# Earlier weight fetches, fewer unread constant products and a direct split of PSUM in the opening of a fused attention and two-layer kernel

## The chip, the cores and the metric

The kernel runs on one core of a Trainium2 chip. The metric is the device time of one execution in microseconds; the figure for the kernel before is the median of three runs. Engines are called as the profile calls them: PE is TensorE, PEld its weight loads, DVE is VectorE, ACT is ScalarE, POOL is GpSimd, and SP is SyncE, which here issues nearly all DMAs.

## What is computed

Causal attention with a bias, then two token-wise layers. Inputs q, k and v are 4 x 8 heads x 576 tokens x 64; the layers are 512 wide with 2048 hidden units, over 2304 tokens, all float32.

```python
bias = -(cum[:, :, :, None] - cum[:, :, None, :])        # cum = cumsum(max(s, 0))
scores = np.where(causal, -1e9, q @ k.T / 8 + np.minimum(bias, 0.0))
attn = softmax(scores)
x = (attn @ v)                       # heads side by side: 2304 x 512
h = x @ w1_in;  x = (h * sigmoid(1.702 * h)) @ w1_out
h = x @ w2_in;  out = (s * max(h, 0)**2 + b) @ w2_out
```

## The kernel before, in words

Float32 operands are split into a rounded part (`hi`, fp32r) and the remainder (`lo`); a product of two split operands is three matmuls. Tokens go in eight units (320 or 256 tokens of one batch). While PE works through the first layer of one unit, the attention of the next unit is woven between its matmuls. The first unit has nothing to be woven into, so its attention stands alone at the start of the program: this opening is where the change lies.

The opening (L540 to L558) runs in steps 0 to 9. In step n PE makes, in this order, the scores of head n in three chunks (`qk`, into `ps`, L311), the values of head n-2 (`pv`, into `po`, L370), and the transposes of head n-1 in two groups (`t`, into `pst`, L349). Behind them DVE masks the scores (L317), ACT takes the exponential (L323), DVE and ACT or POOL normalise (L327, L328, L121, L123), and ACT copies the transposes into `ph` (L353). Only plain float32 is used for the first unit (heads 0 to 7); head 8 is the first of unit 1, and its scores are made from split operands `hi` (L288) and `lo`.

After pv of each head, ACT copies `po` to `xraw` (L384); four `xraw` tiles hold eight heads, two heads each. `split_x` (L424, L425) turns an `xraw` tile into `xT`, whose two planes are the rounded part (ACT) and the remainder (DVE). Just before pv of head 7 PE begins three hidden blocks of the first layer with three of the four `xT` tiles (`h_begin`, 27 matmuls into `ph1`, L438); after it, the last three matmuls of each follow as soon as the fourth tile is there.

Between the pieces of a step PE multiplies a constant tile, `warm`, by itself (`keep_busy`, L201, 128 x 512 bf16 into `bank`); nobody reads the result. `FIRST` such products stand at the start, `FILL` and `EARLY_FILL` say how many precede each piece of a step, and two more stand ahead of each of the hidden blocks 3 to 7 (L458).

Meanwhile the weights come: 16 blocks of `w1i` and then 16 of `w1o`, each 512 KB, by SP (L135). Each one takes ACT and DVE: a sign pass on ACT (L146), a merge of two passes on DVE (L156, L158), and a split (ACT L166, DVE L167). `w1i` has 16 buffers, `w1o` three, so the fourth `w1o` is fetched when the first is split. `next_w1i` and the three calls of `fetch_w` at L555 fix where in SP's order these fetches stand. SP's order and PE's are written out by hand in the opening; those of ACT, DVE and POOL are set by a scheduler when the program is built. All engines execute in order.

SP and ACT issue DMAs on eight completion semaphores in rotation (`DMAHW0` to `DMAHW7` in the order of instructions), and an issue waits there for the DMA that used its semaphore last.

## Time and profile before

| | us |
|---|---|
| median of 3 runs | 1040.61 (1039.55 to 1043.46) |
| the profiled execution | 1039.54 |
| its span | 1037.8 |
| PE busy | 1012.0 (98% of the span) |
| ACT, DVE, POOL busy | 628.1, 609.4, 344.1 |

The 1.7 us between time and span lie around the profiled program. PE is the bound of the whole, so what it loses (idle time, and time in which its clock is granted at half) is what there is to win: in the first 100 us PE is busy for 84.7 us, in the remaining 937.8 us for all but about 10 us. "Idle before" in the rows is time in which an engine had nothing to run, with the instruction whose end released it.

### The profile page before, as it was taken

The numbers are of one execution on the slowest core, as the hardware profiler recorded it, in microseconds if no ns is written. First come the engines' busy times: TensorE is split into PE (matmuls) and PEld (weight loads), VectorE is DVE, ScalarE is ACT, GpSimd is POOL, SyncE is SP. The second block draws the span as 40 slices with busy tenths as digits, with TensorE's granted clock in tenths as the row PEclk, the third lists the DMA queues.
The fourth block names the chain that finished last, engine by engine and source line by source line (L and its number), as shares of the span: only waits on it lengthen the run. The fifth ranks groups of instructions, "written<-read, shape, count | busy, mean of one in ns | idle before, by whom it ended". The sixth has DMA issues, their size and how long they took to land.

```text
span 1037.8 us, 18019 instructions
## 1 busy us (share of the span) xinstructions
PE 1012.0 (98%) x6434; PEld 929.3 (90%) x6434; DVE 609.4 (59%) x1379; ACT 628.1 (61%) x1364; POOL 344.1 (33%) x381
## 2 busy tenths in 40 slices
PE   8978999999999999999999999999999999999998
PEld 3447999999989999999999999899989899999997
DVE  5869766465456677677776565666474334532232
ACT  5968767567538767767767555666455344543342
POOL 1215445345326445445535332011043342311010
PEclk9988999999999999999999999999999999999999
DMA  6766222222022222232222077765126437353321
GB/s 221 241 200 201 66 84 72 57 84 64 8 96 82 83 87 86 73 102 72 86 91 69 15 274 239 253 218 199 46 93 243 158 117 243 111 203 104 119 71 62
DMA packets 52881, 129.60 MB, mean 125 GB/s; under 512 B 7068, under 2 KB 19480, under 8 KB 52792
## 3 DMA queue, kind: packets, MB, share of 16 engines
q1 hardware_dynamic: 52584, 128.32, 37.5%
q8 instruction: 51, 0.84, 0.3%
q14 instruction: 38, 0.31, 0.1%
q10 hardware_dynamic: 208, 0.13, 0.0%
HBM read 95.45 MB, written 28.90 MB: 120 GB/s over the span
## 4 chain that ended last, share of the span: by engine, by line
PE 87%; DVE 4%; DMA 3%; ACT 2%; POOL 1%; issue 1%; SPq 0%; POOLq 0%; DVEq 0%; ACTq 0%
PE py L788 18%; PE ph L438 17%; PE py L480 17%; PE sum_p L762 6%; PE pst L349 5%; PE ph L838 5%; PE ps L311 5%; PE po L376 4%; PE sum_r L762 3%; PE py L729 2%; PE sum_q L762 2%; PE bank L201 1%; DMA pair<-w1o 1%; PE po L370 1%; DMA pair<-w1i 1%
## 5 line engine op out<-in xcount | busy, mean ns | idle before, releaser
L438 PE MATMUL ph<-xT,wi 128*128 128x320 f32 (+1 forms) x1536 | 244.8, 303 | 4.9 <-ACT xT L424 2.0
L788 PE MATMUL py<-wo,g 128*128 128x512 f32 x864 | 223.1, 394 | 0.7 <-DVE g L825 0.7
L438 PEld LDWEIGHTS ph<-xT,wi 128*128 128x128 f32 x1536 | 215.1, 191 | 7.5 <-ACT xT L424 2.2
L480 PE MATMUL py<-g,wo 128*128 128x320 f32 (+1 forms) x1344 | 215.4, 304 | 0.2
L480 PEld LDWEIGHTS py<-g,wo 128*128 128x128 f32 x1344 | 188.1, 189 | 1.2 <-POOL g L467 0.6
L788 PEld LDWEIGHTS py<-wo,g 128*128 128x128 f32 x864 | 160.6, 188 | 26.3 <-DVE g L825 1.0
L467 POOL TENSOR_TENSOR g<-th,g 128x320 fp32r<-128x320 f32 (+1 forms) x128 | 111.1, 869 | 135.1 <-ACT g L466 127.5
L323 ACT ACTIVATE x<-x,m 64x64 f32<-64x64 f32 (+2 forms) x160 | 89.3, 558 | 48.0 <-DVE m L317 47.1
L291 POOL TENSOR_TENSOR lo<-raw,hi 64x576 fp32r<-64x576 f32 (+1 forms) x56 | 68.3, 1220 | 149.5 <-PE ps L311 84.7
L317 DVE CUSTOM_DVE_ANT_0 x<-ps,mask 64x64 f32<-64x64 f32 (+2 forms) x160 | 68.3, 427 | 59.5 <-PE ps L311 58.1
L825 POOL TENSOR_TENSOR g<-odd,g 128x768 fp32r<-128x768 f32 x16 | 30.5, 1907 | 183.3 <-ACT g L822 183.3
L355 ACT ACTIVATE ph<-pst 64x256 fp32r<-64x256 f32 (+2 forms) x144 | 68.4, 476 | 35.6 <-PE pst L349 34.2
L349 PE MATMUL pst<-ident,x 128*128 128x128 f32 (+2 forms) x480 | 82.0, 274 | 1.3 <-DVE ph L358 1.3
L762 PE MATMUL sum_p<-xs,part 128*128 128x384 f32 x384 | 78.5, 339 | 1.4 <-ACT e L860 1.2
L358 DVE TENSOR_TENSOR pl<-pst,ph 128x512 fp32r<-128x512 f32 (+1 forms) x88 | 53.3, 605 | 38.9 <-ACT ph L355 38.4
L762 PEld LDWEIGHTS sum_p<-xs,part 128*128 128x128 f32 x384 | 69.2, 188 | 7.4 <-ACT e L860 1.7
L860 ACT ACTIVATE e<-sum_p 128x384 f32<-128x384 f32 x48 | 23.5, 489 | 84.9 <-PE sum_p L762 84.9
L462 DVE SCALAR_TENSOR_TENSOR th<-th,ph 128x320 f32<-128x320 f32 (+1 forms) x128 | 57.7, 450 | 26.9 <-ACT th L461 25.5
L123 POOL TENSOR_SCALAR x<-x,tot 64x64 f32<-64x64 f32 (+1 forms) x96 | 47.4, 501 | 76.8 <-DVE tot L328 52.3
L466 ACT ACTIVATE g<-th 128x320 fp32r<-128x320 f32 (+1 forms) x128 | 56.1, 438 | 26.3 <-DVE th L462 26.0
L838 PE MATMUL ph<-xs,wi 128*128 128x384 f32 x384 | 71.8, 335 | 0.0
L461 ACT ACTIVATE th<-ph 128x320 f32<-128x320 f32 (+1 forms) x128 | 51.7, 404 | 31.8 <-PE ph L438 30.2
(111 smaller groups left out, 1684.1 us busy)
## 6 DMA issues: line engine op xcount, KB each, us to landing
part<-parts_d SPq DMA_DIRECT2D x32, 512.0 KB
raw<-qkT SPq DMA_DIRECT2D x32, 416.0 KB
pair<-w1i SPq DMA_DIRECT2D x16, 512.0 KB
pair<-w1o SPq DMA_DIRECT2D x16, 512.0 KB
pair<-w2i SPq DMA_DIRECT2D x16, 512.0 KB
pair<-w2o SPq DMA_DIRECT2D x16, 512.0 KB
parts_d<-part SPq DMA_DIRECT2D x16, 512.0 KB
raw<-qkT SPq DMA_DIRECT2D x24, 320.0 KB
```

Of the source, the lines that this page charges most:

```text
L291: nc.gpsimd.tensor_tensor(lo[:D, kc], raw[:D, kc], f32(hi[:D, kc]), ALU.subtract)
L317: nc.vector.tensor_tensor_reduce(out=x[:w, j0:j1], in0=ps[:w, : j1 - j0], in1=mask[:w, WIDE - a0 + j0 : WIDE - a0 + j1], scale=-1.0 / ROOT ...
L323: nc.scalar.activation(x[:w, :a1], x[:w, :a1], AF.Exp, bias=least, scale=-1.0, accum_out=tot[:w, c : c + 1])
L349: nc.tensor.transpose(ps[: j1 - j0, at : at + a1 - a0], t["x"][c][: a1 - a0, j0:j1], ident[: a1 - a0, : a1 - a0])
L355: nc.scalar.activation(t["ph"][:rows, base:end], ps[:rows, :m], AF.Copy)
L438: nc.tensor.matmul(ph[:, :n], wi[f][:, a, cc * P : (cc + 1) * P], x[cc][:, b, :n], start=(k == 0), stop=(k == 3 * NC - 1),)
L462: nc.vector.scalar_tensor_tensor(out=th[:, :n], in0=th[:, :n], scalar=1.0, in1=ph[:, :n], op0=ALU.add, op1=ALU.mult)
L467: nc.gpsimd.tensor_tensor(g[:, 1, :n], th[:, :n], f32(g[:, 0, :n]), ALU.subtract)
L480: nc.tensor.matmul(py[:, :n], wo[f][:, a, wc], g_t[ui, f][:, b, :n], start=(k == 0), stop=(k == 3 * G - 1))
L762: nc.tensor.matmul(ps[:, :N2], w[:, a, c0 : c0 + P], x[kind, k // 3][:, b, :], start=(first and k == 0), stop=(k == 5), skip_group_check=n ...
L788: nc.tensor.matmul(y_sums[t], g2[f % 2][:, a, t * P : (t + 1) * P], wo2[f][:, b, :], start=(first and k == 0), stop=end)
L838: nc.tensor.matmul(ps[:, :N2], wi2[f][:, a, cc * P : (cc + 1) * P], x[f"{cc // 2 + 1}{n + 1}", cc % 2][:, b, :], start=(k == 0), stop=(k = ...
```

## The change

The diff has three parts. `w1i` blocks are fetched one fewer in the set-up and one more after step 0, and the first three `w1o` blocks two steps sooner, after step 5 where they stood after step 7. The constant products are redistributed: 18 in step 1 (20 before), 6 in each step from 2 to 7 (9 before), 6 in steps 8 and 9 (8 before), none ahead of the hidden blocks 3 to 7 (10 before), and 10 after pv of head 7, ahead of the last three matmuls of the first hidden block, into a bank of the transposes: 22 fewer in all, 100 where there were 122. And the values of heads 0 to 7 go from PSUM straight into `xT`: ACT writes the rounded part of 64 x 320, DVE subtracts it from `po`; `xraw` and `split_x` are left out for this unit.

```diff
--- before.py
+++ after.py
@@ -30,7 +30,7 @@
 
 QK_AT, PV_AT, T_AT = (0.05, 0.35), 0.45, (0.55, 0.45)
 SPAN = 0.98
-FIRST, FILL, EARLY_FILL = 30, {"qk": 1, "pv": 2, "t": 2}, {(1, "qk"): 4, (1, "t"): 4}
+FIRST, LAST, FILL, EARLY_FILL = 30, 10, {"qk": (0, 1, 1), "pv": (2,), "t": (1, 1)}, {"qk": (6, 4, 2), "t": (3, 3)}
 EARLY = 1.0
 AHEAD, LEAD = 2, 4
 
@@ -187,7 +187,7 @@
 
         heads = {}
         vs = {}
-        xraw = {}
+        xraw, x0 = {}, []
 
         warm = gp.tile([P, 2 * NMAX], F32, tag="g", name="warm")[:, : C // 2]
         nc.vector.memset(warm, 1.0)
@@ -212,7 +212,7 @@
             raw = t["parts"][0][0]
             nc.sync.dma_start(raw[D + 2 : R, t["kc"]], minus[:2, : u.i1])
             nc.sync.dma_start(raw[D : D + 2, t["qc"]], root[:2, u.i0 : u.i1])
-            next_w1i(2)
+            next_w1i(1)
             for k in range(2):
                 nc.sync.dma_start(rows_d[0, :, 2 + k, :], minus)
                 nc.sync.dma_start(rows_d[1, :, k, :], root)
@@ -375,14 +375,18 @@
                     rhs = t[part][:, at : at + u.n - i]
                     nc.tensor.matmul(po[:, i : u.n], lhs, rhs, start=start, stop=(j == last and part == "ph"))
                     start = False
+            m0 = D * (h % 2)
+            if n < H:
+                if h % 2 == 0:
+                    x0.append(xp.tile([P, 2, NMAX], F32R, tag="xT", name="xT", bufs=4))
+                hi, lo = (x0[-1][m0 : m0 + D, k, : u.n] for k in range(2))
+                nc.scalar.activation(hi, po[:D, : u.n], AF.Copy)
+                nc.vector.tensor_tensor(lo, po[:D, : u.n], f32(hi), ALU.subtract)
+                return
             if h % 2 == 0:
                 xraw[n // H, h // 2] = xp.tile([P, NMAX], F32, tag="xraw", name="xraw")
             x = xraw[n // H, h // 2]
-            m0 = D * (h % 2)
             part = x[m0 : m0 + D, : u.n]
-            if n < H:
-                nc.scalar.activation(part, po[:D, : u.n], AF.Copy)
-                return
             nc.scalar.activation(part, po[D - m0 : 2 * D - m0, : u.n], AF.Copy)
             nc.vector.tensor_tensor(part, po[m0 : m0 + D, : u.n], part, ALU.add)
 
@@ -450,12 +454,12 @@
         def h_item(ui, f, x, between=None):
             n = units[ui].n
             if (ui, f) in begun:
+                if f == 0:
+                    keep_busy(LAST, psT.tile([P, 512], F32, tag="t", name="bank"))
                 ph = begun.pop((ui, f))
                 yield from h_sum(ph, n, f, x, range(NC - 1, NC))
             else:
                 ph = psM.tile([P, 512], F32, tag="m", name="ph1")
-                if ui == 0 and f < G:
-                    keep_busy(2, ph)
                 yield from h_sum(ph, n, f, x, range(NC))
             th = gp.tile([P, NMAX], F32, tag="th", name="th", bufs=2)
             nc.scalar.activation(th[:, :n], ph[:, :n], AF.Tanh, scale=0.851)
@@ -531,7 +535,7 @@
 
         with tc.tile_pool(name="half0", bufs=1, side="right") as pool, tc.manual_schedule(engines={PE}):
             attention_pool(pool, B * H, 0)
-            x0, first_wo = [], []
+            first_wo = []
 
             def next_w1i(n):
                 for f in range(len(wi), min(NF, len(wi) + n)):
@@ -543,15 +547,14 @@
                 for step in range(H + 2):
                     for item in attention_items(step):
                         if item[2] < H and (0, 0) not in begun:
-                            keep_busy(FILL.get(item[1], 0) if step > 1 else EARLY_FILL.get((step, item[1]), 0))
+                            keep_busy((FILL if step > 1 else EARLY_FILL)[item[1]][item[3]] if step else 0)
                         if item[2] == H - 1 and item[1] == "pv":
-                            x0 += [split_x(0, cc) for cc in range(NC - 1)]
                             for f in range(3):
-                                h_begin(0, f, x0)
+                                h_begin(0, f, x0[: NC - 1])
                         if item[2] < H:
                             attend(item)
-                    next_w1i(2)
-                    if step == H - 1:
+                    next_w1i(2 if step else 3)
+                    if step == H - 3:
                         first_wo.extend(fetch_w((pool, "pair", 3), w1o, f) for f in range(3))
                     if step == 1:
                         nc.sync.dma_start(s_sb, s2.partition_broadcast(P))
```

What this does to the instruction orders is shown at three places. In SP's order of the set-up, with the semaphores that each row waits for, before (`pair` is the buffer of a weight block, `raw` that of a head's q and k with the rows of the cumulative sums, `rows_d` their store in DRAM):

```order
L214 DMA raw_156<-root_152 2x320
L135 DMA pair_162<-w1i 128x1024
L135 DMA pair_170<-w1i 128x1024
L217 DMA rows_d_81<-minus_154 32x576
L218 DMA rows_d_81<-root_152 32x576 [waits DMAHW1_49]
L217 DMA rows_d_81<-minus_154 32x576 [waits DMAHW3_49]
L218 DMA rows_d_81<-root_152 32x576 [waits DMAHW4_49]
L230 DMA raw_156<-high_187 1x16x20 [waits DMAHW5_49,DVE_49]
L231 DMA raw_156<-high_187 1x16x20 [waits DMAHW6_49]
L233 DMA rows_d_81<-high_187 32x576 [waits DMAHW7_49]
```

The same place in the changed kernel:

```order
L214 DMA raw_156<-root_152 2x320
L135 DMA pair_162<-w1i 128x1024
L217 DMA rows_d_81<-minus_154 32x576
L218 DMA rows_d_81<-root_152 32x576
L217 DMA rows_d_81<-minus_154 32x576 [waits DMAHW1_49]
L218 DMA rows_d_81<-root_152 32x576 [waits DMAHW3_49]
L230 DMA raw_156<-high_179 1x16x20 [waits DMAHW4_49,DVE_49]
L231 DMA raw_156<-high_179 1x16x20 [waits DMAHW5_49]
L233 DMA rows_d_81<-high_179 32x576 [waits DMAHW6_49]
```

The second weight block has left this stretch, and the two rows from `high` wait for semaphores one place earlier: the first now for a small copy, the second for the first weight block, and none for a second block.

In SP's order after step 5 the piece of the difference with the first `w1o` blocks reads as follows; the row behind them fetches head 7:

```order
+L135 DMA pair<-w1i 128x1024 x2
+L135 DMA pair<-w1o 128x1024 x3
 L268 DMA raw<-qkT 64x640
 L264 DMA raw<-rows_d 4x320
```

The three blocks now stand ahead of the fetches of heads 7, 8 and 9 and of the last two `w1i` blocks.

On ACT, the rows of step 7 of the kernel before that end with the copies of head 6's transposes (`ph`), for which pv of head 6 waits (`hi` here is head 9's, the last row of `pair` ahead of `ph` the sign pass of the first `w1o` block):

```order
L323 ACTIVATE x_683,tot3_74<-x_683,m_686 64x64 [waits DVE_49]
L166 ACTIVATE wi15_664<-pair_659 128x512 [waits DVE_49]
L323 ACTIVATE x_690,tot3_74<-x_690,m_693 128x192 [waits DVE_49]
L323 ACTIVATE x_697,tot3_74<-x_697,m_700 128x320 [waits DVE_49]
L121 ACTIVATE x_617<-x_617,tot2_73 128x320 [waits DVE_49,Activation_49]
L121 ACTIVATE hi_841<-raw_839 128x640 [waits DMAHW1_49]
L384 ACTIVATE xraw_634<-po_710 64x320 [waits PE_49]
L121 ACTIVATE x_697<-x_697,tot3_74 128x320 [waits DVE_49,Activation_49]
L146 ACTIVATE pair_730<-pair_730 128x512 [waits DMAHW3_49]
L353 ACTIVATE ph_717<-pst_718 64x320 [waits PE_49]
L424 ACTIVATE xT_767<-xraw_634 128x320 [waits Activation_49]
L353 ACTIVATE ph_717<-pst_725 128x384 [waits PE_49]
```

And of the changed kernel (`pair_863` is the fourth `w1o` block):

```order
L121 ACTIVATE x_612<-x_612,tot2_73 128x320 [waits DVE_49,Activation_49]
L323 ACTIVATE x_676,tot3_74<-x_676,m_679 64x64 [waits DVE_49]
L166 ACTIVATE wi14_650<-pair_645 128x512 [waits DVE_49]
L323 ACTIVATE x_683,tot3_74<-x_683,m_686 128x192 [waits DVE_49]
L166 ACTIVATE wi15_658<-pair_653 128x512 [waits DVE_49]
L323 ACTIVATE x_690,tot3_74<-x_690,m_693 128x320 [waits DVE_49]
L121 ACTIVATE hi_826<-raw_824 128x640 [waits DMAHW4_49]
L383 ACTIVATE xT_629<-po_703 64x320 [waits PE_49]
L353 ACTIVATE ph_710<-pst_711 64x320 [waits PE_49]
L146 ACTIVATE pair_863<-pair_863 128x512 [waits DMAHW6_49]
L121 ACTIVATE x_690<-x_690,tot3_74 128x320 [waits DVE_49,Activation_49]
L353 ACTIVATE ph_710<-pst_717 128x384 [waits PE_49]
```

A sign pass of a `w1o` block still stands between the two copies; the splits of the first three blocks have moved ahead of this place.

## Rows read from the trace of the kernel before

**Rows 1.** busy time in stretches: us, PE, PEld, DVE, ACT, POOL busy, clock, DMA

```profile
15.00:20.00 5.00, 4.79 (x16) 2.60 (x17) 1.78 (x7) 2.08 (x7) 0.35 (x1) 0.66 0.97 336
...
25.00:45.00 20.00, 20.00 (x99) 10.25 (x98) 16.73 (x53) 19.93 (x53) 2.96 (x6) 1.00 0.81 263
...
60.00:65.00 5.00, 4.20 (x11) 1.52 (x12) 4.59 (x10) 4.30 (x9) 0.00 (x0) 0.50 0.30 120
...
75.00:80.00 5.00, 4.69 (x21) 4.21 (x22) 4.07 (x10) 3.45 (x9) 1.04 (x1) 0.66 0.63 211
...
85.00:90.00 5.00, 2.92 (x20) 2.33 (x18) 4.76 (x9) 3.81 (x10) 2.95 (x4) 1.00 0.75 268
...
95.00:100.00 5.00, 3.15 (x22) 2.80 (x20) 4.88 (x13) 4.53 (x12) 1.24 (x3) 1.00 0.57 172
```

**Rows 2.** timelines of SP, DVE and PE, set-up and step 1

```profile
9.57 0.52 SPq L231 DMA_DIRECT2D raw<-high  x1
...
8.02 0.43 DVE L156 TENSOR_SCALAR pair<-pair 128x512 uint32<-128x512 uint32 x1 [2.20 <-DMA pair<-w1i]
...
1.31 8.41 PE L201 MATMUL bank<-warm 128*128 128x512 bf16 x30 [1.31 <-DVE warm L193]
...
15.21 0.44 PE L311 MATMUL ps<-raw 68*64 68x64 f32 x2 [1.53 <-DMA raw<-rows_d]
```

**Rows 3.** the chain: start, duration, what; a DMA and constant products

```profile
4.70 4.85 DMA pair<-w1i
...
24.26 0.43 PE bank L201 x2
...
63.59 0.97 PE bank L201 x2
```

**Rows 4.** timeline of PE: the first scores of heads 3 and 4

```profile
28.12 0.33 PE L311 MATMUL ps<-raw 68*64 68x64 f32 x2
...
33.72 0.33 PE L311 MATMUL ps<-raw 68*64 68x64 f32 x2
```

**Rows 5.** timeline of ACT: start, duration, line, [idle before <-releaser]

```profile
24.38 0.34 ACT L323 ACTIVATE x<-x,m 64x64 f32<-64x64 f32 x1
...
28.14 0.69 ACT L146 ACTIVATE pair<-pair 128x512 f32<-128x512 f32 x1
...
28.69 0.57 ACT L121 ACTIVATE x<-x,tot 128x320 f32<-128x320 f32 x1
...
56.74 0.74 ACT L121 ACTIVATE hi<-raw 128x640 fp32r<-128x640 f32 x1 [1.42 <-DMA raw<-qkT]
...
59.76 0.68 ACT L146 ACTIVATE pair<-pair 128x512 f32<-128x512 f32 x1 [1.24 <-DMA pair<-w1o]
...
61.01 0.47 ACT L353 ACTIVATE ph<-pst 128x384 f32<-128x384 f32 x1
```

**Rows 6.** timeline of SP: fetch of head 9 and the first w1o blocks

```profile
53.23 0.33 SPq L272 DMA_DIRECT2D raw<-qkT  x1
...
54.67 1.52 SPq L135 DMA_DIRECT2D pair<-w1o  x3
```

**Rows 7.** timeline of PE: pv of heads 6 and 7 and what follows

```profile
60.80 2.79 PE L370 MATMUL po<-ph,vraw 64*64 64x320 f32 x6 [3.45 <-ACT ph L353]
...
71.00 1.54 PE L370 MATMUL po<-ph,vraw 64*64 64x320 f32 x6
...
74.55 0.41 PE L438 MATMUL ph<-xT,wi 128*128 128x320 f32 x1 [2.00 <-ACT xT L424]
...
75.31 0.99 PE L438 MATMUL ph<-xT,wi 128*128 128x320 f32 x5 [0.36 <-DVE xT L425]
```

**Rows 8.** single lines: durations in ns, minimum/median/maximum

```profile
L424 ACT ACTIVATE xT<-xraw x32: 401/435/473, 35.0 to 598.3; 128x320 fp32r<-128x320 f32 x16, 128x256 fp32r<-128x256 f32 x16
...
L387 DVE TENSOR_TENSOR xraw<-po,xraw x56: 396/427/495, 106.3 to 597.3; 64x256 f32<-64x256 f32 x32, 64x320 f32<-64x320 f32 x24
```

**Rows 9.** the weight buffers: DVE's split of a w1o block

```profile
L167 DVE TENSOR_TENSOR wo<-pair,wo x16: 662/692/1519, 63.3 to 111.2; 128x512 fp32r<-128x512 f32 x16
```

## The prediction, made before the changed kernel ran

> **What bounds the kernel now.** I read the busy times first: PE fills 98% of the span, so only what PE loses counts, and nearly all of that lies in the first 105 us. The busy time in stretches [rows 1] shows it twice: as idle time of PE (2.1 of 5 us from 85 on, 1.8 of 5 from 95 on), and in the column of the clock, 0.66, 0.50 and 0.66 in the stretches from 15, 60 and 75 us, where a part or all of the time ran at 1.2 instead of 2.4 GHz. From 25 to 45 us PE is busy for 20.00 us of 20 and at full clock, but so is ACT, for 19.93: two engines are full at once, and a part of PE's work there is constant products.
>
> Next I read who PE waits for. It waits 1.53 us for head 1's rows at 15.21 [rows 2], 3.45 us for ACT's copy of head 6's transposes at 60.80, and 2.00 and 0.36 us for the last tile of `xT` at 74.55 and 75.31 [rows 7]. Each of these waits ends just before, or within, a stretch of low clock.
>
> Then I asked why ACT was late at 60.80. ACT's rows [rows 5] show 1.42 and 1.24 us of waiting for DMAs at 56.74 and 59.76; the last is the sign pass of the first `w1o` block, which stands ahead of the copy. SP issued that block at 54.67, behind head 9's fetch at 53.23 [rows 6], which is held until head 7's scores are done.
>
> **The set-up.** In the chain the first two weight blocks take until 9.55 (4.70 + 4.85) [rows 3], and SP's second row from `high` starts at 9.57 [rows 2]: by the order it waits for the second block's semaphore. In the changed order it waits for the first block's. DVE's merge of that block began at 8.02 [rows 2], so I take 8.0 for the issue, and all behind it is 1.6 us earlier; head 1's scores start at 13.6 instead of 15.21. The constant products at the start end at 9.72 (1.31 + 8.41) in either kernel, so of the two waits around head 0 (9.72 to the rows from `high`, and the 1.53) one is closed. I therefore take the low clock of the stretch from 15 us as gone: 0.66 over 5 us is 3.4 us at half, worth 1.7 us. Step 1 has two constant products fewer: a pair takes 0.43 us at full clock [rows 3], 0.4. PE and ACT reach head 2 at most 1.6 + 1.7 + 0.4 = 3.7 us sooner. Three weight blocks in a row now arrive ahead of head 2's fetch; if head 2 waits for them, the lead is as little as 1.6.
>
> **Steps 2 to 7.** A step takes 5.6 us (28.12 to 33.72) [rows 4]. Three constant products fewer make 0.65 us of PE's step, but ACT is as full, and ACT is what remains. So these 18 products are worth nothing by themselves: what they free, PE waits. I count ACT's work instead, from head 2's first exponential at 24.38 to the second copy of head 6's transposes at 61.01 [rows 5]. Of the DMA waits in it (2.7 us) the 1.24 falls away, since three `w1o` blocks are there long before, and the 1.42 falls away, since other work has moved ahead of it. Added are eight passes over weights (four signs, four splits by the new order; the starts 28.14 and 28.69 give 0.55 each, 4.4 us), and three splits from `xraw` are gone (0.435 us each, 1.3) [rows 8]. Thus 3.1 of work against 2.7 of waits, and a lead of 3.7 becomes 3.3 at head 6's pv. The early `w1o` blocks also stand ahead of head 7's fetch and of two `w1i` blocks: 2.5 MB behind one another at the 263 GB/s of the stretch [rows 1] are nearly two steps. I take 0.5 us of new waits on ACT for it (from 0 to the whole lead), and keep **2.8**.
>
> DVE's eight subtractions from PSUM are nearest to the row of `xraw` with 64 partitions, 0.43 us, against four of 128 partitions before, some 1.5 us more; DVE is busy for 16.73 us of 20 there [rows 1], so ACT covers it. Without that cover it is 1.5 us. `po`, of which there is one, is held 0.4 us longer; the next pv is a step away.
>
> **From pv of head 6 to the first hidden block.** PE still waits for the copy, some 3 us, because ACT has become the limit; I keep the half clock behind it. Two constant products fewer until `h_begin` are a pair at half clock, 0.97 us [rows 3]: **1.0**. After pv of head 7 PE went from 72.54 (71.00 + 1.54) to 75.31 until the second of the last products [rows 7]. Now ten constant products fill 2.15 us, in which ACT's one copy and DVE's one subtraction (0.43 each) end; the same point comes 2.3 us after pv, **0.5** sooner. Since PE does not stop there, the low clock of the stretch from 75 is gone too, again 3.4 us at half: **1.7**. What covers those ten is the copy's latency; if ACT is busy with `w1o` passes instead, they cost up to 2.15 on top of the old wait.
>
> **The hidden blocks 3 to 7.** Ten constant products leave. Six of them run ahead of the stretch from 85 us, where PE has no wait but that at 74.55: **1.3**. The other four run in it, beside waits for DVE, and are worth nothing. From 85 to 100 DVE is busy 4.76 and 4.88 us of 5 [rows 1]: the merges and splits of `w1o` fill it. By the new order two more blocks than before have passed ACT when the first hidden block's activation comes; a block's split takes 0.69 us [rows 9], the first of its two merge passes 0.43 [rows 2], and the second I take like the split: some 1.8 us, so that 3.6 us of DVE work for the two leave the window. Of the 2.1 and 1.8 us of PE's idle time in it I take **1.5** back (0 to 3.9).
>
> **The sum.** 2.8 + 1.0 + 0.5 + 1.7 + 1.3 + 1.5 = 8.8 us. The profiled execution took 1039.5; the changed one would take 1030.7. The median of the runs is 1.1 above the profiled execution, so I forecast 1031.8 for it. Behind 105 us PE is full in both kernels, so the lead should last.
>
> **Rivals.**
> *The wait only moves.* The copy for head 6 still stands behind a sign pass of a `w1o` block, now the fourth, and this one too is issued behind head 9's fetch, which waits for head 7's scores. If ACT arrives there early, it waits for the DMA as before: head 7's scores plus 7.6 us (53.23 to 60.80 [rows 6, 7]), with perhaps 1.5 less, since two blocks are in flight instead of three. Together with late weight blocks in steps 2 to 7 the lead of 2.8 is gone, the low clock of 75 stays, and DVE's window gives nothing: 1.0 + 0.5 + 1.3 = 2.8, so 1037.8 for the median. For it speaks the order; against it, that ACT's own work up to that place has grown by 3.1 us, so that it comes late anyhow.
>
> *Everything goes.* If ACT keeps pace and PE's wait at pv of head 6 is short, the clock stays up there: 60 to 65 at 0.50 is 2.5 us more. With all of DVE's window (2.4 more) and no new waits (0.5), the gain is 14.2: 1026.4.
>
> *Slower: the clock in steps 2 to 7.* PE's 20.00 us of 20 at clock 1.00 come with nine constant products a step; with six, PE waits for ACT in every step. A step then holds 5.6 - 0.65 = 4.95 us of PE work, against some 5.4 of ACT (an estimate: 5.6 less the 0.2 of half a split from `xraw`). At half clock for three quarters of the time the work takes 4.95 / 0.625 = 7.9; six steps at 2.5 more than 5.4 cost 15 us, 6 more than the forecast gains: 1046.8. It decides from three fifths of the time, where a step takes 7.1 and the gain is eaten. Against it: the falls to half clock in the trace follow waits of 1.5 us and more, and the new ones should share some 0.45 us a step. The Trainium skill has a rule on this side: the page "TensorE: Matmul & The Clock Gate", in the section "A second HAM failure mode: psum-queue depth-cycling", describes a kernel in which frequent small gaps between groups of matmuls let the clock swing between its two levels. By that rule this rival would be the likelier one; PE has no such gaps from 25 to 45 us in this trace, so nothing here tests it.
>
> **How the numbers follow.** Half a percent, 5.2 us, is about what a measurement of this kernel tells from no change: faster is under 1035.4, slower over 1045.8. The forecast (a gain of 5.2 to 12) has 0.60. The gain of over 12 has 0.15. The moved wait has 0.17 and counts as no change. The clock in steps 2 to 7 has 0.08, most of it slower. The range leaves out that one and the ends of the next: from 1025.0, just past the whole gain, to 1038.5, just past the moved wait. The forecast's own range is 1027.5 to 1035.4.
>
> **What the new profile would show.** Right: head 1's first scores near 13.6; clock 1.00 from 15 to 20 us and again from 75 to 80 us of the old time; ACT full in steps 2 to 7 and PE with short waits for `ph` in each; pv of head 6 near 57.8 and of head 7 near 67; less idle PE before the first `py`. Wrong: a clock below 1.00 between 20 and 45 us; ACT waiting for `w1o` or `w1i` for over 1 us ahead of a copy; head 7's or head 8's scores waiting for their fetch; or a lead at 105 us that has shrunk by the end of the span.

## The result, and the profile after

The changed kernel takes **1047.62 us** (1045.75 to 1047.91, 6 runs) against 1040.57 for the kernel before beside it, a ratio of **1.0062 [1.0044, 1.0080]**: slower, where 1031.8 was forecast and 1038.5 was the range's upper end. The profiled execution has a span of 1045.8 us (1037.8 before) at a mean granted clock of 0.979 (0.990 before).

The busy time of the changed kernel in stretches, with the columns of [rows 1]:

```profile
15.00:20.00 5.00, 3.83 (x20) 2.15 (x18) 3.18 (x10) 3.70 (x11) 0.88 (x2) 1.00 1.01 323
20.00:25.00 5.00, 3.42 (x10) 1.91 (x10) 2.58 (x8) 3.58 (x10) 0.23 (x1) 0.69 0.86 268
25.00:30.00 5.00, 5.00 (x14) 2.17 (x14) 3.19 (x9) 2.34 (x6) 0.00 (x0) 0.50 1.02 337
...
40.00:50.00 10.00, 8.70 (x43) 4.66 (x43) 9.55 (x30) 9.95 (x27) 1.49 (x2) 1.00 0.96 326
50.00:55.00 5.00, 3.14 (x13) 1.59 (x13) 5.00 (x13) 5.00 (x13) 2.28 (x2) 0.76 0.83 299
55.00:75.00 20.00, 15.12 (x42) 6.88 (x41) 14.55 (x31) 11.85 (x28) 7.76 (x7) 0.50 0.42 134
...
80.00:85.00 5.00, 5.00 (x29) 2.88 (x27) 3.25 (x6) 2.38 (x5) 0.00 (x0) 1.00 0.47 168
```

The low clock of 15 to 20 us is gone; a new one stands at 20 to 30 and a long one, 20 us at half, at 55 to 75. The timeline of PE, which answers to [rows 2] and [rows 7]:

```profile
14.12 0.30 PE L311 MATMUL ps<-raw 68*64 68x64 f32 x2 [0.52 <-DMA raw<-rows_d]
...
21.58 0.30 PE L311 MATMUL ps<-raw 68*64 68x64 f32 x2 [2.75 <-DMA raw<-qkT]
...
25.29 2.79 PE L370 MATMUL po<-ph,vraw 64*64 64x320 f32 x6
...
49.89 1.51 PE L370 MATMUL po<-ph,vraw 64*64 64x320 f32 x6 [0.66 <-DVE xT L384]
...
52.38 0.24 PE L349 MATMUL pst<-ident,x 64*64 64x64 f32 x1 [0.65 <-POOL x L123]
53.83 0.63 PE L349 MATMUL pst<-ident,x 128*64 128x128 f32 x2 [1.22 <-POOL x L123]
...
59.40 2.80 PE L370 MATMUL po<-ph,vraw 64*64 64x320 f32 x6
...
70.34 2.77 PE L370 MATMUL po<-ph,vraw 64*64 64x320 f32 x6 [4.88 <-ACT ph L353]
...
80.39 1.54 PE L370 MATMUL po<-ph,vraw 64*64 64x320 f32 x6
81.86 2.33 PE L201 MATMUL bank<-warm 128*128 128x512 bf16 x10
83.84 1.23 PE L442 MATMUL ph<-xT,wi 128*128 128x320 f32 x6
...
92.93 1.96 PE L442 MATMUL ph<-xT,wi 128*128 128x320 f32 x8 [2.96 <-DVE th L466]
```

Head 1's scores start 1.1 us sooner, but head 2's wait 2.75 us for their rows, so pv of head 0 (25.29) is 0.7 us later than before. Pv of head 6 stands at 70.34 where it stood at 60.80, and of head 7 at 80.39 (71.00). Behind that the kernels run nearly alike: of the 9.4 us 8.0 are left in the spans.

The chain names what head 2 waits for, its own fetch behind three weight blocks:

```profile
13.97 7.52 DMA raw<-qkT
```

And the timelines of SP, POOL and ACT show who is late ahead of pv of head 6:

```profile
52.52 9.67 SPq L278 DMA_DIRECT2D vraw<-vP  x2
62.73 0.34 SPq L272 DMA_DIRECT2D raw<-qkT  x1
...
51.50 2.28 POOL L123 TENSOR_SCALAR x<-x,tot 64x64 f32<-64x64 f32 x2 [6.85 <-PE po L370]
55.94 4.19 POOL L123 TENSOR_SCALAR x<-x,tot 64x64 f32<-64x64 f32 x2 [2.16 <-PE ps L311]
60.11 0.50 POOL L123 TENSOR_SCALAR v<-vraw 128x384 fp32r<-128x384 f32 x1
...
66.63 0.74 ACT L121 ACTIVATE hi<-raw 128x640 fp32r<-128x640 f32 x1 [5.57 <-DMA raw<-qkT]
```

In the changed program the scheduler put head 6's two normalising passes (`x`) ahead of head 8's `v` on POOL; before, `v` came first. Here the two passes take 4.19 us, `v` starts at 60.11, SP stands for 9.67 us at the next `vraw`, whose buffer `v` must free, head 9's fetch is issued at 62.73 (53.23 before, [rows 6]), and ACT, in order, waits 5.57 us for it ahead of the copy that pv of head 6 needs. This change of order on POOL, which the diff does not show, is called **the flip**.

The long stretch of half clock begins ahead of the flip:

```profile
52.00:53.00 1.00, 0.24 (x1) 0.10 (x1) 1.00 (x3) 1.00 (x4) 1.00 (x2) 0.81 1.02 388
```

From 53 us on the clock is 0.50. No long wait stands there: PE waited 0.66 us for DVE's subtraction (`xT`) and 0.65 and 1.22 us for POOL's passes of head 5, which take 2.28 us. The 4.88 us wait lies within the half clock that had already come.

### The profile page after: what moved, and what is told of

Same layout as the page of the kernel before. It is cut to its first block, busy times and chain, and to the rows that moved or that the text cites. A ratio compares the mean times of both kernels' runs of the same rounds, so it can differ in the third digit from the quotient of the medians.

```text
span 1045.8 us, 17967 instructions
## 1 busy us (share of the span) xinstructions
PE 1015.4 (97%) x6412; PEld 931.8 (89%) x6412; DVE 608.9 (58%) x1383; ACT 627.0 (60%) x1360; POOL 344.7 (33%) x381
## 4 chain that ended last, share of the span: by engine, by line
PE 86%; DVE 5%; DMA 3%; ACT 3%; issue 1%; POOL 1%; SPq 0%; DVEq 0%; ACTq 0%; POOLq 0%
PE py L791 18%; PE ph L442 18%; PE py L484 17%; PE sum_p L765 6%; PE ph L841 5%; PE pst L349 5%; PE ps L311 5%; PE po L376 4%; PE sum_r L765 3%; PE py L732 2%; PE sum_q L765 2%; DMA pair<-w1i 1%; DMA pair<-w1o 1%; PE bank L201 1%; DVE hi L290 1%
## 5 line engine op out<-in xcount | busy, mean ns | idle before, releaser
L123 POOL TENSOR_SCALAR x<-x,tot 64x64 f32<-64x64 f32 (+1 forms) x96 | 50.6, 534 | 77.7 <-DVE tot L328 57.5
```

## The experiments

The parts of the change are called **fetch** (`w1i`: one block in the set-up, three after step 0), **early w1o**, **products** (the constant ones) and **split** (direct from PSUM). The theories: **Q**, three weight blocks ahead of head 2's fetch; **V**, the flip; **F**, the products missing from the steps let the clock fall by themselves; **W**, the early `w1o` fills ACT and DVE; later **T** (the tail's products), **G** and **H** (below). Each result gives the median of the run (and that of the kernel before beside it, where it changes from the last one given), the ratio, and the mean granted clock over its runs (before: 0.992 to 0.993 in each set).

**Without the fetch.**

```diff
-            next_w1i(1)
+            next_w1i(2)
-                    next_w1i(2 if step else 3)
+                    next_w1i(2)
```

> The changed kernel with the first part of its fetch schedule undone: two w1i blocks in the set-up and two after step 0, as before. Theory Q (three weight blocks in a row ahead of head 2's fetch make PE wait 2.75 us and put it at half clock for some 10 us): the wait for head 2 and the low clock from 22 to 32 us are gone, pv of head 1 starts near 30 instead of 33.3, and the time falls by 4 to 6 us for this alone. In this build POOL also takes head 8's v ahead of head 6's normalisation again, so theory V (that order holds up SP and head 9's fetch) gives another 4 to 5: 1037 to 1040 by both, 1042 to 1044 by Q alone. Theory F (too few constant products let the clock fall) expects 1046 to 1048 as the constant products stay as changed.

1043.52 against 1039.84, 1.0028 [1.0015, 1.0042], clock 0.986. The flip is gone here too, so by both theories it should have been 1037 to 1040: a miss. The wait for head 2 is gone and the clock is 1.00 up to 40 us, as Q wants; but it now falls between 40 and 70 us, and the time does not follow.

**Without the early w1o.**

```diff
-                    if step == H - 3:
+                    if step == H - 1:
```

> The changed kernel with the first three w1o blocks fetched after step 7 again. In this build POOL takes head 8's v first. Theory Q: the wait of 2.75 us for head 2 stays, with the half clock behind it. Theory V: SP is not held at the fetch of a third vraw for 9.7 us, ACT does not wait 5.6 us for head 9; 1041 to 1043. If the early w1o blocks are what costs by themselves (theory W: they fill ACT and DVE between 45 and 62 us), under 1040. Theory F: 1046 to 1048.

1040.83, 1.0012 [0.9995, 1.0030], clock 0.985. The time lies between V's range and W's. The wait for head 2's rows is still there (2.25 us), yet the profile has clock 1.00 up to 40 us: the wait is not enough for the fall. The flip is gone here as well.

**Head 6's normalising passes on DVE.**

```diff
-                engine = nc.scalar if k == last else nc.gpsimd
+                engine = nc.scalar if k == last else nc.vector if n == H - 2 else nc.gpsimd
```

> The changed kernel with one edit: the two small passes that normalise head 6 run on DVE instead of POOL. All orders up to there are as in the changed kernel; POOL has nothing ahead of head 8's v. Theory V: v of head 8 is split some 4 us sooner, SP's wait at the third vraw falls from 9.7 to 4 us or less, ACT's wait for head 9 from 5.6 to under 2, pv of head 6 starts at 64 to 67 instead of 70.3, and the time falls by 3 to 6 us: 1042 to 1044. Theory Q and theory F: the stage up to 52 us is the same, so the time is 1046 to 1048.

1041.72, 1.0009 [0.9993, 1.0024], clock 0.987. Its profile, of the slowest of its ten runs (1044.26):

```profile
61.88 2.80 PE L370 MATMUL po<-ph,vraw 64*64 64x320 f32 x6
69.83 2.77 PE L370 MATMUL po<-ph,vraw 64*64 64x320 f32 x6 [1.89 <-DVE xT L384]
...
54.70 5.76 SPq L278 DMA_DIRECT2D vraw<-vP  x2
...
68.07 0.68 ACT L146 ACTIVATE pair<-pair 128x512 f32<-128x512 f32 x1 [2.18 <-DMA pair<-w1o]
```

SP stands 5.76 us instead of 9.67 at `vraw`, and head 9's rows no longer hold ACT. Pv of head 6 starts 7.95 us behind that of head 5, where it was 10.94: 3.0 us sooner. It stands at 69.83 all the same and not at 64 to 67, since this execution was 2.5 us late before that, and ACT now waits 2.18 us for a `w1o` block ahead of the copy, which is the wait of the prediction's first rival. By the medians 5.5 us of the changed kernel's time hang on head 6's passes on POOL (0.0053 of 1040; with both intervals, 3 to 8). So V holds for the stage and for most of the loss, though two of its signs were missed. The edit takes the flip away and, with it, the slow passes; it does not tell the two apart. Some 1 us of loss and about half of the lost clock are left.

**Without the products.**

```diff
-                            keep_busy((FILL if step > 1 else EARLY_FILL)[item[1]][item[3]] if step else 0)
+                            keep_busy(FILL.get(item[1], 0) if step > 1 else EARLY_FILL.get((step, item[1]), 0))
-                if f == 0:
-                    keep_busy(LAST, psT.tile([P, 512], F32, tag="t", name="bank"))
+                if ui == 0 and f < G:
+                    keep_busy(2, ph)
```

(with the numbers of `FILL` and `EARLY_FILL` as before)

> The changed kernel with the constant products as before (122 of them, two ahead of the hidden blocks 3 to 7, none after pv of head 7). In this build POOL takes head 8's v first. Theory F: the clock stays up from 22 us on and the time is 1038 to 1041. Theory Q: the wait of 2.75 us for head 2 stays and so does the fall of the clock, as no constant product stands in that wait; with the POOL order gone 1041 to 1044.

1038.59, 0.9986 [0.9973, 0.9999], clock 0.992. With the products back there is no flip, head 2 waits 0.38 us and the clock is full from 20 to 50 us. F stood best at this point, and the second set was to test it.

**The products alone**, on the kernel before:

```diff
-                            keep_busy(FILL.get(item[1], 0) if step > 1 else EARLY_FILL.get((step, item[1]), 0))
+                            keep_busy((FILL if step > 1 else EARLY_FILL)[item[1]][item[3]] if step else 0)
-                if ui == 0 and f < G:
-                    keep_busy(2, ph)
+                if f == 0:
+                    keep_busy(LAST, psT.tile([P, 512], F32, tag="t", name="bank"))
```

(with the changed numbers of `LAST`, `FILL` and `EARLY_FILL`)

> The kernel before with the changed constant products alone: fetches, w1o and the split of x as before. In the written order POOL again does head 6's two normalising passes ahead of head 8's v. Theory F (the products missing from steps 2 to 7 let the clock fall by themselves): mean granted clock below the kernel before by about half as much as the changed kernel's, 0.985 against 0.993, and the time at 1042 to 1047, the later end if POOL's order holds SP as well. Rival (the products are free as long as the fetches are the old ones): clock at 0.992 or more and 1038 to 1040, the hidden blocks' products saved. If the clock is unhurt between 20 and 52 us and falls only from 52 on, POOL's order is to blame and not the products.

**1035.29 against 1039.43, 0.9949 [0.9930, 0.9968]**, clock 0.9925. F falls: alone, the missing products cost nothing and gain 4 us, and this in spite of the flip, which the order of this kernel has too. The timeline of its PE and two stretches:

```profile
22.57 1.54 PE L370 MATMUL po<-ph,vraw 64*64 64x320 f32 x6
27.52 1.54 PE L370 MATMUL po<-ph,vraw 64*64 64x320 f32 x6
32.47 1.54 PE L370 MATMUL po<-ph,vraw 64*64 64x320 f32 x6
...
46.55 0.81 PE L311 MATMUL ps<-raw 68*128 68x320 f32 x2 [2.55 <-DVE m L317]
...
55.73 1.54 PE L370 MATMUL po<-ph,vraw 64*64 64x320 f32 x6
...
59.02 0.75 PE L370 MATMUL po<-ph,vraw 64*64 64x320 f32 x2
59.99 0.86 PE L370 MATMUL po<-ph,vraw 128*64 128x256 f32 x4 [0.23 <-ACT ph L353]
...
48.00:54.00 6.00, 6.00 (x19) 3.07 (x18) 3.10 (x10) 4.87 (x13) 3.51 (x5) 0.50 0.59 151
...
60.00:70.00 10.00, 10.00 (x57) 7.04 (x57) 7.17 (x14) 6.92 (x13) 0.00 (x0) 1.00 0.47 162
```

The kernel before, at pv of heads 2 and 5:

```profile
35.81 1.54 PE L370 MATMUL po<-ph,vraw 64*64 64x320 f32 x6
...
53.56 1.54 PE L370 MATMUL po<-ph,vraw 64*64 64x320 f32 x6
```

Steps 2 and 3 take 4.95 us here, where they took 5.60 [rows 4]: exactly the three products fewer. In the steps, PE waits for over 1 us only from 35 us on. The lead is 3.3 us at pv of head 2; at pv of head 5 it is gone (2.2 us later than before), behind the wait of 2.55 us and some 6 us of half clock. It returns at pv of head 6, which starts 1.8 us sooner with hardly a wait (0.23 us for 3.45 [rows 7]) and at full clock, where the kernel before runs at half (0.50 from 60 to 65 [rows 1]).

**The hidden blocks' products kept**, the steps' changed:

```diff
-                if f == 0:
-                    keep_busy(LAST, psT.tile([P, 512], F32, tag="t", name="bank"))
+                if ui == 0 and f < G:
+                    keep_busy(2, ph)
```

(`LAST` is left out)

> The changed kernel, but in the hidden blocks 0 to 7 the two constant products each as before, and not ten ahead of block 0; the products of the steps stay changed. POOL's order is that of the changed kernel. Theory F: this half of the change of products is not what costs, so the time stays near the changed kernel's 1047 (1045 to 1049) and the clock near 0.979. Rival T (the loss comes from the tail, where ten products stand in one place and none in the blocks after): back to 1039 to 1042.

1041.80, 1.0034 [1.0011, 1.0058], clock 0.987. Neither: its runs go from 1038.9 to 1050.5, at a clock of 0.990 to 0.995 in the five below 1041.4 and of 0.975 and 0.976 in the two above 1050. POOL's order is flipped; the time goes with the clock.

**The steps' products kept**, the hidden blocks' changed:

```diff
-                            keep_busy((FILL if step > 1 else EARLY_FILL)[item[1]][item[3]] if step else 0)
+                            keep_busy(FILL.get(item[1], 0) if step > 1 else EARLY_FILL.get((step, item[1]), 0))
```

(with the numbers of `FILL` and `EARLY_FILL` as before)

> The changed kernel, but the constant products of the attention steps as before; the hidden blocks have ten ahead of block 0 and none after, as changed. POOL's order is that of the kernel before. Theory F: clock 0.992 or more, full between 20 and 50 us, and 1037.5 to 1039, by up to the predicted 1.3 us faster than with all the products back (1038.6). Rival T: the low clock comes back and the time is 1041 or more.

1039.59, 0.9994 [0.9979, 1.0009], clock 0.992. The mean clock is whole again, so T falls (in the profiled execution it is 0.66 from 20 to 30 us, behind a wait of 1.40 us for head 2's rows, and 1.00 from there to 60). But the products taken out of the hidden blocks and put after pv of head 7 gain nothing over having them as before (1038.59).

**Fetch and split alone.**

```diff
-                    if step == H - 3:
+                    if step == H - 1:
```

(and all products as before)

> The kernel before with the w1i blocks fetched one in the set-up and three after step 0, and the first unit's x split directly; constant products and the first w1o fetch as before. Against the run with all products back it differs in the first w1o fetch alone. Theory W (the early w1o blocks fill ACT and DVE in steps 6 and 7 and cost what they give): 1036 to 1038.5, not slower than with them. Rival, by the prediction's terms (the w1o blocks two steps sooner take the wait of 1.24 and part of DVE's window away): 1040 to 1042, 1.5 to 3 us slower than the run with all products back.

1036.37, 0.9970 [0.9954, 0.9986], clock 0.993: two parts that gain together, and the time that W gave; its rival falls.

**Products and split.** The fetches as before.

```diff
-            next_w1i(1)
+            next_w1i(2)
-                    if step == H - 3:
+                    if step == H - 1:
```

> The changed products and the direct split, with the weight fetches of the kernel before. The products alone gave 1035.3. By the count of ACT's passes the split takes 1.3 us off ACT ahead of head 6's pv, so theory G (from 20 to 55 us ACT sets the pace; a lead gained ahead of it turns into waits of PE and then into half clock) gives 1033.5 to 1036, a little below the products alone. Theory Q (the changes hurt one another only where head 2's fetch stands behind three weight blocks) gives the same, since that fetch is as before. Rival: the split itself is what goes badly with fewer products (DVE's subtractions from PSUM stand ahead of the scores' maxima): 1038 or more.

1039.40 against 1039.36, 1.0007 [0.9995, 1.0019], clock 0.9865. The rival comes out: beside fewer products the split costs 4 to 5 us (the products alone: 1035.29, and 1035.07 below), with the lower clock.

**The third block later** (on the run without the early `w1o`, so no flip):

```diff
-                    next_w1i(2 if step else 3)
+                    next_w1i(3 if step == 3 else 2)
```

> As the changed kernel with w1o late, but the w1i block moved out of the set-up is fetched after step 3 and not after step 0, so that two blocks, not three, stand ahead of head 2's fetch. With three it took 1040.8. Theory Q: no wait of PE for head 2's rows over 0.5 us, clock 1.00 up to 45 us, 1033 to 1036. Theory G: PE only reaches ACT earlier and waits there, the clock falls between 35 and 60 us instead, 1038.5 to 1041.5.

1039.01, 0.9996 [0.9981, 1.0012], clock 0.989. Head 2's wait is 0.29 us, as Q wants, and the clock is 1.00 to 50 us in the profiled run; but the median is G's. The profiled execution is the fastest of the twelve (1034.57), so the rows show its best case. Even there PE waits 1.95 us at 37.87 and 1.81 at 51.85 for the scores' maxima: the lead turns up as waits further on.

**The early w1o alone**, on the kernel before:

```diff
-                    if step == H - 1:
+                    if step == H - 3:
```

> The kernel before with the first w1o blocks two steps sooner and nothing else. By the prediction's terms (the wait of 1.24 us ahead of head 6's copy gone, 1.5 us of DVE's window back, less 3.1 us of new work on ACT that a wait of 1.42 partly covers): 1037 to 1040. Theory W (the three blocks' sign and split passes fill ACT and DVE ahead of head 6's copies, where nothing else covers them): 1040.5 to 1043, pv of head 6 later than 60.80 or no sooner.

1039.23, 1.0003 [0.9990, 1.0017], clock 0.993. No gain and no loss. W's time did not come (its sign did: pv of head 6 starts at 61.92, 1.1 us later than before, with a wait of 1.73 instead of 3.45), and the prediction's gain did not either: 1039.23 lies in its range, but the kernel before beside it took 1039.36.

**Fetch and products.** The split and `w1o` as before.

```diff
-            next_w1i(2)
+            next_w1i(1)
-                    next_w1i(2)
+                    next_w1i(2 if step else 3)
```

(and the edits of the products alone)

> The changed w1i fetch and the changed products, with w1o and the split as before. With the split as changed this took 1040.8, and the products without the fetch 1035.3. Theory Q: 1040 to 1043, with a wait of about 2 us for head 2's rows and half clock within 20 us behind it. Rival (the direct split is what costs beside fewer products): 1035 to 1037.

1037.03, 0.9983 [0.9968, 0.9998], clock 0.987. The time is the rival's: without the split this pair still gains. But it gains 2 us less than the products alone, at the lower clock, so the fetch costs something beside them too.

**The changed kernel with nine products a step again from step 4 on**, and then **in steps 2 and 3 instead**. Both leave POOL's order as it was before, and all else as changed, so they differ in the place and in how many come back: 14 late, 6 early.

```diff
+FULL = {"qk": (1, 1, 1), "pv": (2,), "t": (2, 2)}
-                            keep_busy((FILL if step > 1 else EARLY_FILL)[item[1]][item[3]] if step else 0)
+                            keep_busy((FULL if step > 3 else FILL if step > 1 else EARLY_FILL)[item[1]][item[3]] if step else 0)
```

> The changed kernel, with the constant products of steps 4 to 9 as before (nine a step) and those of steps 1 to 3 as changed. POOL's order is that of the kernel before. So far the clock fell (mean 0.979 to 0.987) only where the steps' products had left and something else of the change came with it. Theory H: it falls where PE has caught up with ACT and DVE, from about 38 us on, and waits 1 to 5 us at a time; with nine products from step 4 on those waits shrink: clock at 0.990 or more, 1037 to 1040. Theory Q (three weight blocks ahead of head 2's fetch with three products fewer at that place): a wait of 2 us and more at head 2's scores and low clock behind it as in the changed kernel, 1041 to 1044.

**1037.30 against 1040.02, 0.9976 [0.9962, 0.9990]**, clock 0.992.

```diff
+                            keep_busy((FILL if step > 3 else FULL if step > 1 else EARLY_FILL)[item[1]][item[3]] if step else 0)
```

> The other half: the changed kernel, with nine constant products in steps 2 and 3 as before and six from step 4 on. POOL's order is that of the kernel before. Theory H: the waits from 38 us on stay, the clock falls there, mean 0.984 to 0.988, 1041 to 1044. Theory Q: head 2's wait is as in the kernel with all products back, the clock stays up to 50 us, mean 0.990 or more, 1037 to 1040.

1042.29, 1.0009 [0.9994, 1.0025], clock 0.984. Both times are H's, and Q falls. That the number and not the place decides is not tested: no run puts back 14 early or 6 late. Back late, in stretches:

```profile
20.00:30.00 10.00, 9.11 (x26) 4.42 (x26) 5.76 (x16) 5.79 (x15) 0.00 (x0) 0.56 0.98 313
...
40.00:50.00 10.00, 9.20 (x46) 4.89 (x47) 9.62 (x31) 9.95 (x26) 1.72 (x2) 1.00 1.00 325
50.00:60.00 10.00, 8.48 (x39) 4.07 (x41) 9.97 (x26) 9.95 (x25) 4.62 (x7) 1.00 0.59 189
```

Back early:

```profile
20.00:30.00 10.00, 9.72 (x45) 5.00 (x46) 9.33 (x30) 9.57 (x25) 1.47 (x2) 1.00 0.93 310
...
40.00:50.00 10.00, 6.36 (x22) 3.35 (x20) 9.02 (x26) 9.80 (x24) 5.08 (x4) 0.76 0.78 273
50.00:60.00 10.00, 9.01 (x31) 4.34 (x31) 6.64 (x19) 6.90 (x18) 2.36 (x3) 0.73 0.69 214
```

The first kernel waits 1.94 us for head 2's rows and loses the clock behind it, and is still faster than the kernel before; what it keeps is the clock from 40 to 60 us, which the second loses behind this wait of PE, with POOL's passes that it is for:

```profile
44.45 0.24 PE L350 MATMUL pst<-ident,x 64*64 64x64 f32 x1 [3.49 <-POOL x L124]
...
40.67 4.12 POOL L124 TENSOR_SCALAR x<-x,tot 64x64 f32<-64x64 f32 x2 [6.80 <-PE po L371]
```

The profiled executions lie towards opposite ends of their runs (1040.47 with the products back late, 1039.41 early), so the verdict is that of the medians and the mean clocks; the rows show where.

**Fetch and products with the late products back**, and **products alone with the late ones back** (two earlier kernels, both with this edit):

```diff
-                            keep_busy((FILL if step > 1 else EARLY_FILL)[item[1]][item[3]] if step else 0)
+                            keep_busy((FULL if step > 3 else FILL if step > 1 else EARLY_FILL)[item[1]][item[3]] if step else 0)
```

> The changed w1i fetch and the changed products, with nine products again from step 4 on; w1o and the split as before. Without those it took 1037.0 at a mean clock of 0.987, with low clock from 40 to 55 us. Theory H: those falls go (0.9 us of products come back for each step, which PE spends instead of waiting), mean clock 0.991 or more, 1033 to 1036. If the low clock from 40 us has another cause, 1036.5 to 1039.

1039.27, 1.0003 [0.9986, 1.0020], clock 0.991. A miss: two thirds of the lost clock came back, the time did not (1037.03 without). PE waits 2.19 and 2.81 us for ACT's copies at 59.81 and 63.37 instead.

> The changed products alone, with nine again from step 4 on. The products alone took 1035.3 at a clock of 0.9925, so little low clock can be won back, and four steps' savings go. Theory H: 1035 to 1037.5, no better than with six products throughout. If fewer products from step 4 on cost more than they save here too: 1032.5 to 1034.5.

1038.70, 0.9988 [0.9973, 1.0002], clock 0.993: slower than with six products throughout, and slower than H said. Where the mean clock holds anyhow, products put back cost what they take: 14 of them are 3.0 us at 0.43 a pair, and the gain fell from 4.1 and 4.8 us to 1.3.

**The late products back, without the early w1o**:

```diff
-                    if step == H - 3:
+                    if step == H - 1:
```

> The changed kernel with nine constant products again from step 4 on and with the first w1o fetch as before. With the early w1o this took 1037.3. Without products put back, leaving out the early w1o was worth 5.8 us (part of it the order on POOL), and with all products in place some 2. If the early w1o costs ACT and DVE time by itself: 1033.5 to 1036. If it matters only through POOL's order, which is that of the kernel before in both: 1037 to 1039.

1038.38, 0.9990 [0.9972, 1.0008], clock 0.9915. With POOL's order the same, the early `w1o` makes no difference that these runs can tell (0.9990 and 0.9976), so the first of the two cases falls.

**The products alone, again**:

> The changed constant products alone, a second time, since the first result (1035.3, clock 0.9925) is the fastest so far and rests on the fewest runs. If the products are worth the 0.65 us a step that PE's rows showed (pv 4.95 us apart instead of 5.60 in steps 2 to 4), 1034 to 1036.5; if the first result was a lucky set of runs, 1038 to 1040.

1035.07 against 1039.85, **0.9956 [0.9941, 0.9971]**, clock 0.9925: confirmed, and the fastest version; it beats both kernels.

## Why the prediction was wrong

**The step that failed** is "So these 18 products are worth nothing by themselves: what they free, PE waits." It is wrong twice. Alone, PE did not wait at first: steps 2 and 3 became 0.65 us shorter, and the products gained 4.1 and 4.8 us. And beside the other parts taking them out is not free. Put back whole, they bring the changed kernel from 1.0062 to 0.9986, 7.9 us and more than the whole loss: 5.5 us is what goes with the flip, which comes and goes with them here, and some 2.4 us (with both intervals, 0.3 to 4.5) lies between two kernels without it (1.0009 and 0.9986), with the clock at 0.987 and 0.992. The rival that says so, "Slower: the clock in steps 2 to 7", had 0.08 and 1046.8; the changed kernel took 1047.6. That the numbers agree is chance, since most of the loss hangs on POOL's order, which the rival does not have. Its mechanism was right in kind and wrong in place: not a wait of 0.45 us in each step, but one of 2.75 us for a fetch at head 2, and then waits of 0.65 to 1.22 us around 52 us, where PE has caught up with DVE and POOL, with 4.88 us more inside the half clock. With the products back from step 4 on, the change is faster than the kernel before. This takes the flip away as well; against the run without the flip (1.0009) the late products are worth 3.4 us (1.3 to 5.6).

**How much goes with the clock.** Within the kernels tried (194 runs, each beside its own kernel's mean), 0.01 of mean granted clock goes with 6.0 us (least squares). From 0.993 to the 0.979 of the changed kernel that makes 8.3 us; the median lost 7.05. A loss of this size is thus what such a fall goes with. It is not shown that the clock alone makes it: a run with more waits is longer by the waits themselves too.

**The flip** was not foreseen at all: 5.5 us by the run with DVE. It lengthens the fall and does not start it: the half clock begins between 52 and 53 us, ahead of the flip, and ends only behind the 4.88 us wait. It did no such harm in the products alone, which have it too: their POOL passes take 1.25 us at that place instead of 4.19.

**The set-up** was right in its times: 14.12 for 13.6, clock 1.00 from 15 to 20 us, and head 2 waited behind three blocks, as the text's last sentence there allows. The 1.7 us for the clock rested on one execution, though. In the early `w1o` alone, whose set-up and wait at head 1 (1.56 us) are those of the kernel before, the profiled execution has full clock at this place anyway:

```profile
15.00:20.00 5.00, 4.76 (x24) 2.64 (x25) 2.44 (x9) 2.67 (x8) 0.33 (x1) 1.00 0.96 293
```

And the lead at pv of head 0, which here is 0.7 us the wrong way, decides little: the run with the third block later has 3.6 us there in its profile (21.02 against 24.62), and by the medians 0.4 us in all, which is no change.

**ACT and the weights, "from 0 to the whole lead"** at 0.5 us: the upper end came. ACT and DVE are busy 5.00 of 5 us from 50 to 55, and a lead that arrives there is waited away. The split, whose added subtractions on DVE were costed at nothing under ACT's cover, is not free once products are missing: products and split together are 4 to 5 us slower than the products alone. That it is the subtractions is argued and not shown; PE waits there for DVE's maxima (1.82 us at 39.58) and for POOL's passes (1.44 and 1.97 us at 44.06 and 52.95).

**After pv of head 7** the ten products did what was said: the last three products of the first block follow without a wait, the first 3.45 us after pv's start (3.55 before, and another wait behind it, [rows 7]), and the clock is 1.00 from 80 to 85.

**The hidden blocks**: 1.3 and 1.5 us were forecast, nothing came. With the ten products moved ahead of the first block the time is that with them as before (1039.59, 1038.59), as PE waits for DVE's `th` instead: 2.14 and 2.28 us, against 0.86 and 2.01. And the early `w1o` alone gains nothing (1.0003); PE still waits 2.96 us for DVE's `th` at 92.93.

**The page weighed there**, "TensorE: Matmul & The Clock Gate" of the Trainium skill, section "A second HAM failure mode: psum-queue depth-cycling", by which the rival would have been the likelier, pointed to the right side. The traces agree only in part. In the changed kernel the long fall comes among waits of 0.66, 0.65 and 1.22 us. But in the kernel of fetch and products, waits of 0.3 to 1.3 us stand among full clock up to 38 us, and with the steps' products kept three of 0.93 to 1.22 us, from 49 to 55 us, leave it full up to 60.

**What stays open**: why the half clock behind the 2.55 us wait of the products alone lasts some 6 us and that of the changed kernel, from 53 us on, over 20, and why the late products help the full change but neither fetch and products nor the products alone. No run separates these.

## What to carry over

A filler product can be taken out at no cost only where nothing hangs on it, and it may be what keeps the clock up at that place: look for where PE will catch up with its suppliers, and try thinning the fill ahead of that point and behind it separately. In the full change the fill behind it was worth keeping; in two smaller changes it was not. Gains of parts do not add: the products gained 4 to 5 us alone, fetch and split 3 together, the early `w1o` nothing, and all of them lost 7. A low clock seen in one execution may be missing from the next: do not count its end as a gain before a second trace shows it. And compare the order that a scheduler gives to engines which the edit does not touch.

## What was not expected of the hardware

POOL's two 64 x 64 normalising passes take 0.71 to 2.03 us in the opening of the kernel before, up to 4.19 in the changed one, and up to 6.08 in the run without the fetch, while DVE runs weight passes with hardly a gap:

```profile
37.66 6.08 POOL L123 TENSOR_SCALAR x<-x,tot 64x64 f32<-64x64 f32 x2 [2.16 <-ACT pair L146]
```

In the kernels with the split the longest pair takes 1.72 to 6.08 us, in those without it 1.50 to 3.38. The Trainium skill's page "SBUF — State Buffer", section "SBUF: two separate sides", says that DVE and GpSimd share a pair of ports as an exclusive lock, so that an operation of GpSimd and one of DVE that uses the pair (in a 2-port mode, or with two inputs in SBUF) block each other whole. The rows fit that; no run here takes DVE's passes away to prove it.

Head 2's fetch, 160 KB, took 7.52 us behind three blocks of 512 KB in the changed kernel. In the same place of the order it took at most 6.3 us with the products back (issued at 13.93, scores at 20.25), and behind two blocks at most 5.6 (13.37 and 18.95, the third block later).
